# Trial matrix products of 64 rows, in pairs on the two halves of the array, behind the last projection

## The chip, the cores and the metric

The kernel runs on one core of one Trainium2 chip. That core has a matrix engine (PE, an array of 128 rows by 128 columns, which loads a 128-column weight tile and then streams up to 512 columns of a second operand past it), a vector engine (DVE), a scalar engine (ACT), a third elementwise engine (POOL), and a queue that issues most of the transfers (SP). Products are summed in PSUM, which has 8 banks of 128 partitions by 512 float32.

The metric is the time of one execution on the device in microseconds. Two executions of the kernel before took 689.73 and 689.46 us, a median of 689.6 us. The profile shown below belongs to the second of them.

## The reference

The result is the sum of the input, an attention branch and a gated feed-forward branch, both fed from the same layer norm. There are 2048 tokens of width 448, 16 heads of 28, four segments of 512 tokens, and a hidden width of 1792.

```
xn = layernorm(x)
# branch A: softmax attention inside each of 4 segments, plus a recurrent memory over the segments
q, k, v = xn @ wq, xn @ wk, xn @ wv                  # 16 heads of 28
for s in range(4):
    p = softmax(q_s @ k_s.T * scale + mask)          # mask falls on keys behind the query
    o_s = g * (phi(q_s) @ M) / (phi(q_s) @ z + 1e-6) + (1 - g) * (p @ v_s)
    M, z = M + phi(k_s).T @ v_s, z + sum(phi(k_s))
A = o @ wo
# branch B
B = (sigmoid(xn @ w_gate) * (xn @ w_up)) @ w_down
return x + A + B
```

## The kernel before

Every dense product is made to float32 accuracy from operands split in two: a high part rounded to the type `float32r`, and a low part with the rest. A product is then summed from terms high x high, high x low and low x high. The contraction of 448 is cut into three chunks of 128 and one of 64; of the last one the transposed activations hold the high part on partitions 0 to 63 and, beside it, on partitions 64 to 127, the same chunk's low part. With that packing one dense product takes the 11 terms of the table `TERMS`: nine for the three whole chunks and two for the packed one. Each term is one matrix product over all 128 rows of the array, and the 11 add up in one PSUM bank (`start` on the first, `stop` on the last).

`xs[b]` holds the split and transposed activations of token block b: 128 partitions, 7 slices of 512 columns. There are four such tiles. At the end of the program, `split_tokens` has overwritten them with the attention's output.

The work comes in this order. A front part makes the layer norm, the values (`pv`, line 335), the keys and queries (`pp`, line 355) and the memory. Then the feed-forward branch (`pgu`, line 247; `pd`, line 173) and the attention (scores `st`, line 612; weighted values `pa`, line 687) run interleaved on the matrix engine, in an order that the program writes out by hand for PE and SP (`tc.manual_schedule(engines=MANUAL)`). Last comes `project()`: the output projection `po` (line 771), 16 groups of 11 terms, each of 448 columns. Behind each group DVE adds the bank to the residual `acc` (line 775) and SP stores 128 tokens to the output (line 776). The last instruction of PE in the program is the eleventh term of the sixteenth `po`.

PSUM is shared out by tags: `"p"` and `"gu"` have two banks each, and `bank(name, tag)` hands them out in turn. The projection takes `"p"` and `"gu"` alternately. A bank that is handed out again is waited for until whoever used it last is done. Two kinds of product in the kernel before don't fill the array: `st` has 84 rows, and `pa` has 32 columns; four `pa` products at a time stand beside each other on four column strips of the array, and go to four strips of partitions in one bank. `pa` has plain float32 operands, for which the engine runs each product as two passes. No product of the kernel before has 64 rows.

Of the kernel before, what the change touches and what calls it, by code (L numbers as in the profile page):

```python
# [16 lines left out]
P = 128  # L17
D = 448
# [4 lines left out]
L = 512  # L23
# [38 lines left out]
def kernel(  # L62
# [11 lines left out]
    V, A, G, T = nc.vector, nc.scalar, nc.gpsimd, nc.tensor  # L74
# [6 lines left out]
    xs = [keep.tile([P, 7, L], F32R, name=f"xs{b}") for b in range(NB)]  # L81
# [194 lines left out]
    with tc.tile_pool(name="front", bufs=2) as sb, tc.manual_schedule(engines=FRONT):  # L276
# [227 lines left out]
        for b in range(NB):  # L504
            last = b == NB - 1
# [23 lines left out]
            for k, c in enumerate((3, 4, 5, 6, 0, 1, 2) if last else range(7)):  # L529
# [34 lines left out]
                n = k - 1 if b == 0 else k + 1  # L564
# [135 lines left out]
    def attention():  # L700
        for n in range(2):
            pairs[n].load()
        units[0].load_values()
        yield
        run, behind = {}, []
        for u in range(len(units) + 1):
            for n in range(2):
                run[n] = pairs[2 * u + n].scores() if u < len(units) else iter(())
            for k, which in enumerate(SLOT):
                if u == len(units):  # L710

                    if k > 9:
                        break
                    which = (None,) * 8 + (2, 3)
                    which = which[k]
                if behind:
                    next(behind.pop(0))
                if which is not None and which < 2 and u < len(units):
                    next(run[which])
                    n = 2 * u + which + 2  # L720
                    if which not in SLOT[k + 1:]:
                        behind += [run[which]] * PARTS
                        if n < len(pairs):
                            pairs[n].load()
                        else:
                            load_sums(n - len(pairs))
                if which == 2 and u > 0:
                    fin = units[u - 1].finish()
                    next(fin)
                    if u < len(units):  # L730
                        units[u].load_values()
                if which == 3 and u > 0:
                    next(fin)
                yield
# [14 lines left out]
    def project():  # L749

        def split_tokens(b, t):
            o3 = sums[b][:, :, t * P:(t + 1) * P]
            A.activation(xs[b][:, 0:4, t * P:(t + 1) * P], o3, AF.Copy)
            transpose_low(o3, xs[b], t)

        def out_weights(w):
            at = 2 * D * (w // 4) + D * (w % 2)
            return wo[w % 4 // 2][:, at:at + D]

        yield  # L760
        for n in range(NB * NT + 2):
            if n < NB * NT:
                b, t = divmod(n, NT)
                split_tokens(b, t)
                if t == NT - 1 and b + 2 < NB:
                    load_sums(b + 2)
            if n >= 2:
                b, t = divmod(n - 2, NT)
                po = bank("po", ("p", "gu")[n % 2])
                for m, (a, w) in enumerate(TERMS):  # L770
                    T.matmul(po[:, :D], xs[b][:, a, t * P:(t + 1) * P], out_weights(w),  # L771
                             start=m == 0, stop=m == len(TERMS) - 1)
                    if m in (3, 7):
                        yield
                V.tensor_add(acc[b][:, t, :], po[:, :D], acc[b][:, t, :])
                nc.sync.dma_start(out[b * L + t * P:b * L + (t + 1) * P, :], acc[b][:, t, :])
                yield
                if rest:
                    yield from rest.pop(0)

    N_OUT = 1 + NB * NT * 3 + 12
    steps = attention()
    n_att = len(units) * len(SLOT) + 10
    done = 0
    with tc.manual_schedule(engines=MANUAL):
        next(steps)
        k = sum(FILLS) + 6
        for part in (ffn, project()):
            for _ in part:
                want = min(round(n_att * (k - LEAD) / (N_FFN + N_OUT - LEAD - TAIL)), n_att)  # L790
                k += 1
                while done < want:
                    next(steps)
                    done += 1


def _rows(w):
# [36 lines left out]
```

## Time and profile before

| | |
|---|---|
| time of the profiled execution | 689.46 us |
| span from its first to its last instruction | 687.7 us |
| so outside the span | 1.8 us |
| PE busy | 681.7 us, 99% of the span, 3594 matrix products |
| DVE, ACT, POOL busy | 567.4, 342.6, 151.3 us |
| granted clock of PE | 0.999 of full speed |

Of the matrix engine the profile has two rows per product: PE is the streaming, PEld is the load of its weight tile, which goes on beside the product before. A record of PE is longer than the place it takes in the row of products: products are pipelined, so their records overlap, and what one costs is the distance between starts of neighbours. Names in a row read out<-in; `128*128 128x512` means 128 rows by 128 columns of the array and 512 columns streamed. The lines that carry the argument stand with it below.

### The profile page before, as it was taken

The numbers are of one execution on the slowest core, as the hardware profiler recorded it, in microseconds if no ns is written. First come the engines' busy times: TensorE is split into PE (matmuls) and PEld (weight loads), VectorE is DVE, ScalarE is ACT, GpSimd is POOL, SyncE is SP. The second block draws the span as 40 slices with busy tenths as digits, with TensorE's granted clock in tenths as the row PEclk, the third lists the DMA queues.
The fourth block names the chain that finished last, engine by engine and source line by source line (L and its number), as shares of the span: only waits on it lengthen the run. The fifth ranks groups of instructions, "written<-read, shape, count | busy, mean of one in ns | idle before, by whom it ended". The sixth has DMA issues, their size and how long they took to land.

```text
span 687.7 us, 10438 instructions
## 1 busy us (share of the span) xinstructions
PE 681.7 (99%) x3594; PEld 566.6 (82%) x3594; DVE 567.4 (83%) x994; ACT 342.6 (50%) x563; POOL 151.3 (22%) x349
## 2 busy tenths in 40 slices
PE   8999999999999999999999999999999999999997
PEld 7898888778878787787878878787787878878897
DVE  6765795767788988998898989989898899889863
ACT  4837555343554555543655446454653565446320
POOL 3500020101223222232332222322322322222000
PEclk9999999999999999999999999999999999999999
DMA  7446556696233323243223252314333332423342
GB/s 267 181 150 238 198 214 242 249 330 174 71 94 92 80 86 86 56 128 112 56 64 107 57 141 56 109 47 116 82 94 77 96 71 64 95 79 95 95 153 106
DMA packets 45796, 84.37 MB, mean 123 GB/s; under 512 B 6320, under 2 KB 20400, under 8 KB 45232
## 3 DMA queue, kind: packets, MB, share of 16 engines
q1 hardware_dynamic: 42736, 76.37, 35.8%
q0 software_dynamic: 3008, 7.34, 4.9%
q8 instruction: 28, 0.46, 0.3%
q14 instruction: 24, 0.20, 0.1%
HBM read 51.05 MB, written 32.64 MB: 122 GB/s over the span
## 4 chain that ended last, share of the span: by engine, by line
PE 70%; DVE 14%; issue 9%; POOL 4%; DMA 1%; ACT 1%; SPq 0%; POOLq 0%; ACTq 0%
PE pgu L247 26%; PE pd L173 13%; PE pp L355 10%; PE po L771 5%; PE pv L335 5%; PE st L612 3%; PE pa L687 3%; DVE mx L629 3%; DVE w L666 2%; POOL w L627 2%; DVE acc L174 2%; PE pmm L383 2%; PE n L401 2%; DVE hh L259 1%; DVE mx L633 1%
## 5 line engine op out<-in xcount | busy, mean ns | idle before, releaser
L247 PE MATMUL pgu<-xs,wgu 128*128 128x512 f32 x1232 | 304.1, 394 | 0.0
L247 PEld LDWEIGHTS pgu<-xs,wgu 128*128 128x128 f32 x1232 | 228.2, 188 | 47.4 <-issue 2.2
L173 PE MATMUL pd<-wdn,hh 128*128 128x448 f32 x672 | 156.0, 367 | 0.0
L627 POOL TENSOR_SCALAR_AFFINE_SELECT w<-w 128x256 f32<-128x256 f32 (+1 forms) x160 | 81.2, 509 | 236.4 <-ACT w L616 183.6
L173 PEld LDWEIGHTS pd<-wdn,hh 128*128 128x128 f32 x672 | 122.5, 188 | 12.3 <-issue 0.6
L667 ACT ACTIVATE w<-w 128x1024 f32<-128x1024 f32 (+1 forms) x96 | 87.3, 915 | 65.0 <-DVE w L666 64.2
L666 DVE TENSOR_TENSOR w<-w,mb 128x1024 f32<-128x1024 f32 (+1 forms) x96 | 98.9, 1045 | 0.1
L616 ACT ACTIVATE w<-st 128x512 f32<-128x512 f32 x128 | 74.9, 590 | 45.3 <-PE st L612 44.9
L629 DVE TRANSPOSE_TENSOR_REDUCE mx<-w 128x32 f32<-128x1024 f32 x64 | 79.0, 1235 | 17.0 <-POOL w L627 17.0
L355 PE MATMUL pp<-xs,wqk 128*128 128x512 f32 x308 | 77.7, 401 | 0.0
L174 DVE TENSOR_TENSOR acc<-pd,acc 128x448 f32<-128x448 f32 x112 | 67.1, 599 | 1.2 <-PE pd L173 1.1
L355 PEld LDWEIGHTS pp<-xs,wqk 128*128 128x128 f32 x308 | 56.8, 188 | 13.4 <-issue 2.4
L258 ACT ACTIVATE hh<-sg 128x512 fp32r<-128x512 f32 x56 | 35.2, 628 | 56.4 <-DVE sg L256 49.3
L612 PE MATMUL st<-qk 84*128 84x128 f32 (+3 forms) x256 | 61.9, 312 | 0.0
L255 ACT ACTIVATE sg<-pgu 128x512 f32<-128x512 f32 x56 | 33.2, 594 | 49.4 <-PE pgu L247 49.2
L612 PEld LDWEIGHTS st<-qk 84*128 84x128 f32 x256 | 47.6, 189 | 6.9 <-ACT w L616 0.3
L656 DVE STREAM_TRANSPOSE mb<-top 128x1024 f32<-128x1024 f32 x32 | 39.8, 1242 | 10.5 <-POOL top L653 10.1
L362 DVE TENSOR_TENSOR qk<-pp,qk 128x512 fp32r<-128x512 f32 x28 | 19.3, 688 | 29.8 <-ACT e L360 23.7
L259 DVE SCALAR_TENSOR_TENSOR hh<-sg,hh 128x512 fp32r<-128x512 f32 x56 | 38.7, 691 | 2.6 <-ACT hh L258 2.4
L335 PE MATMUL pv<-wv,xs 128*128 128x448 f32 x176 | 39.6, 376 | 0.4 <-DVE xs L102 0.3
L687 PE MATMUL pa<-w,vv 128*32 128x128 f32 (+3 forms) x512 | 39.7, 436 | 0.2
L256 DVE SCALAR_TENSOR_TENSOR sg<-sg,pgu 128x512 f32<-128x512 f32 x56 | 37.3, 665 | 1.8 <-PE pgu L247 1.6
(100 smaller groups left out, 640.6 us busy)
## 6 DMA issues: line engine op xcount, KB each, us to landing
qk<-qd SPq DMA_DIRECT2D x192, 112.0 KB
qd<-qk SPq DMA_DIRECT2D x28, 512.0 KB
raw<-in_w_ffn SPq DMA_DIRECT2D x14, 512.0 KB
vd<-vst SPq DMA_DIRECT2D x4, 1024.0 KB
vv<-vd SPq DMA_DIRECT2D x16, 256.0 KB
od<-w POOLq DMA_DIRECT2D x16, 256.0 KB, 3.8
sums<-od SPq DMA_DIRECT2D x32, 128.0 KB
out<-acc SPq DMA_DIRECT2D x16, 224.0 KB
```

The costliest lines, as they stand in the source:

```text
L173: T.matmul(pd[:, :D], l, r, start=n == 0, stop=n == len(mms) - 1)
L174: V.tensor_add(acc[b][:, t, :], pd[:, :D], acc[b][:, t, :])
L247: T.matmul(dst, wgu[f][:, w, side * P:(side + 1) * P], xs[b][:, a, :], start=n == 0, stop=n == len(TERMS) - 1)
L335: T.matmul(pv[:, :D], xs[b][:, a, t * P:(t + 1) * P], wv[w], start=n == 0, stop=n == len(TERMS) - 1)
L355: T.matmul(pp, wqk[c][:, w, :], xs[b][:, a, :], start=n == 0, stop=n == len(TERMS) - 1)
L612: T.matmul(st[:, at:at + L - kb * P], self.qk[:KS, 1, h, kb * P:(kb + 1) * P], self.qk[:KS, 0, h, kb * P:], start=True, stop=True)
L616: A.activation(w, st, AF.Copy)
L627: G.affine_select(d, d, pattern=pattern, base=0, channel_multiplier=-1, compare_op=ALU.is_ge, fill=MASK)
L629: V.tensor_reduce(mx[:, 16 * (n - 1):16 * (n + 1)], w3[:, n // 2, :2 * L].rearrange("p (b n) -> p b n", n=32), axis=mybir.AxisListType.X, ...
L666: V.tensor_sub(w, w, m)
L667: A.activation(w, w, AF.Exp, scale=SCALE)
L687: T.matmul(pa[32 * j:32 * j + 32, kb * P:], self.vv[:, kb, 32 * j:32 * j + 32], self.pairs[j // 2].block(j % 2, kb), start=kb == 0, stop=k ...
```

## The change

A function `trials()` is added and called once, behind the loops that issue everything else. It issues matrix products on PE and nothing on any other engine. Their weights are slices of `xs[1]`, their streamed operand slices of `xs[0]`, and their results stay in PSUM: nothing reads them, and the output is computed as before.

There are 17 blocks. Nine of them (`ta`, `tc`, `te`, `tg`, `ti`, `tk`, `tm`, `to`, `tq`) are made by `plain`: four products over all 128 rows, into one bank. The eight between them are made by `halves`: pairs of products of 64 rows, one of each pair on rows 0 to 63 and one on rows 64 to 127, each half with a bank of its own. The blocks of halves differ in how many pairs they have, in the width (512 or 448 columns), in the offset of the streamed slices (0, 16 or 32 columns), in whether the lower or the upper half comes first (`swap`), and in whether they use one pair of banks or two in turn.

```
+    def trials():
+        f0, f1 = (xs[b].rearrange("p c n -> p (c n)") for b in range(2))
...
+        def col(cols, k, off=0):
+            at = off + k % (6 if cols == L else 7) * cols
+            return f0[:, at:at + cols]
+
+        def wt(k):
+            return f1[:, k % 27 * P:k % 27 * P + P]
+
+        def plain(name, tag, reps, cols=L):
+            o = bank(name, tag)[:, :cols]
+            for n in range(reps):
+                T.matmul(o, wt(n), col(cols, n), start=n == 0, stop=n == reps - 1)
+
+        def halves(name, plan, cols=L, off=0, swap=False):
+            tags = ("gu", "p", "gu", "p") if len(plan) > 1 else ("gu", "p")
+            outs = [bank(name, t)[:, :cols] for t in tags]
+            reps, last, k = {}, {}, 0
+            for n, a, b in plan:
+                for o in (a, b):
+                    reps[o] = reps.get(o, 0) + n
+            seen = dict.fromkeys(reps, 0)
+            for n, a, b in plan:
+                begun = dict(last)
+                for m in range(n):
+                    for h in ((1, 0) if swap else (0, 1)):
+                        o = (a, b)[h]
+                        r = slice(64 * h, 64 * h + 64)
+                        i = T.matmul(outs[o], wt(2 * k + h)[r], col(cols, k, off)[r],
+                                     start=seen[o] == 0, stop=seen[o] == reps[o] - 1).ins
+                        if m == 0 and o in begun:
+                            tc.add_manual_dep(i, begun[o].name, sync, reason="half")
+                        seen[o] += 1
+                        last[o] = i
+                    k += 1
+
+        whole = ((11, 0, 1), (11, 2, 3))
+        plain("ta", "p", 4)
+        halves("tb", ((16, 0, 1),))
+        plain("tc", "p", 4)
+        halves("td", whole)
+        plain("te", "p", 4)
+        halves("tf", whole, swap=True)
+        plain("tg", "p", 4)
+        halves("th", ((16, 0, 1),), L, 16)
+        plain("ti", "p", 4)
+        halves("tj", ((16, 0, 1),), L, 32)
+        plain("tk", "p", 4, D)
+        halves("tl", ((14, 0, 1),), D, 0)
+        plain("tm", "p", 4, D)
+        halves("tn", ((14, 0, 1),), D, 16)
+        plain("to", "p", 4, D)
+        halves("tp", ((4, 0, 1),))
+        plain("tq", "gu", 4)
...
+        trials()
```

The order of the other engines stays what it was. On PE, all new rows stand between the last projection and the end of the program. The first of them (`x32` counts products, so 16 pairs):

```order
 L771 MATMUL po<-wo,xs_67 128x448 x44
 L771 MATMUL po<-wo,xs_68 128x448 x44
-L830 UNCONDITIONAL_BRANCH
+L797 MATMUL ta<-xs_65,xs_66 128x512 x4
+L813 MATMUL tb<-xs_65,xs_66 128x512 x32
+L797 MATMUL tc<-xs_65,xs_66 128x512 x4
+L813 MATMUL td<-xs_65,xs_66 128x512 x44
+L797 MATMUL te<-xs_65,xs_66 128x512 x4
+L813 MATMUL tf<-xs_65,xs_66 128x512 x44
+L797 MATMUL tg<-xs_65,xs_66 128x512 x4
```

Nothing in front of `ta` has moved; the program's end on PE now stands behind 284 more products (36 plain ones, 248 of halves).

Inside a block of halves, PE's row in the changed kernel alternates between the two banks of a pair. This is the place in `td` where the second pair of banks takes over (the numbers at the names are those of the banks' tiles: 7092 and 7094 belong to rows 0 to 63, 7093 and 7095 to rows 64 to 127; a wait named PE is one for a product that this engine itself issued earlier):

```order
L813 MATMUL td_7092<-xs0_65,xs1_66 128x512
L813 MATMUL td_7093<-xs0_65,xs1_66 128x512
L813 MATMUL td_7094<-xs0_65,xs1_66 128x512
L813 MATMUL td_7095<-xs0_65,xs1_66 128x512 [waits PE_49]
L813 MATMUL td_7094<-xs0_65,xs1_66 128x512
L813 MATMUL td_7095<-xs0_65,xs1_66 128x512
```

The bank of 7095 was last written by `tc`, 22 products earlier. There are 17 such waits in the new rows, each for a bank whose last product lies at least four products back.

More of the change, by code (lines that the diff above doesn't have):

```diff
@@ L779, in project @@
                     yield from rest.pop(0)
+    def trials():
+        f0, f1 = (xs[b].rearrange("p c n -> p (c n)") for b in range(2))
+        sync = mybir.DependencyInfo(mybir.DependencyClass.Sync, mybir.DependencyReason.DATA)
+        def col(cols, k, off=0):
[46 more added lines that the diff above has]
+        plain("tq", "gu", 4)
     N_OUT = 1 + NB * NT * 3 + 12
```

## The prediction

> **What bounds the kernel now.** I read the page first, then the chain of work that ended last near its end, then single rows of the timeline. The page's line of busy times and its line of the granted clock:
>
> ```profile
> PE 681.7 (99%) x3594; PEld 566.6 (82%) x3594; DVE 567.4 (83%) x994; ACT 342.6 (50%) x563; POOL 151.3 (22%) x349
> PEclk9999999999999999999999999999999999999999
> ```
>
> PE is busy almost throughout and its clock is granted in full from end to end. What the change appends comes at the end, so that is the place to read. The chain of work that ended last, from 640 us to the end (start, length, engine, line, count):
>
> ```profile
> 641.46 1.21 PE pd L173 x6
> 642.66 2.29 PE pa L687 x32
> 644.96 2.41 PE po L771 x11
> ...
> 651.96 2.20 PE po L771 x11
> 654.16 1.20 PE pd L173 x6
> ...
> 662.16 22.01 PE po L771 x110
> 684.17 0.02 issue
> 684.20 0.62 DVE acc L775
> ```
>
> The chain at the end is PE alone: product behind product, without a wait. 110 products of 448 columns take 22.01 us, 0.200 us each. PE sets the end until 684.17. Whatever is appended to PE's row starts there and moves the end, except for what lies beside the tail that follows anyway. That tail:
>
> ```profile
> 683.80 0.36 PE L771 MATMUL po<-wo,xs 128*128 128x448 f32 x1
> 684.20 0.62 DVE L775 TENSOR_TENSOR acc<-po,acc 128x448 f32<-128x448 f32 x1 [1.57 <-PE po L771]
> ...
> 684.85 0.33 SPq L776 DMA_DIRECT2D out<-acc  x1
> ...
> SPq L830 <- DMA out<-acc: 1.2, 1, 1.2
> ...
> L830 SPq DRAIN  x3: 7/7/7, 686.9 to 687.2; - x3
> ...
> L830 PEldq DRAIN  x2: 13/1900/3788, 680.4 to 687.3; - x2
> L830 DVEq DRAIN  x2: 19/342/664, 684.2 to 687.3; - x2
> ```
>
> The last product starts at 683.80. Then come the add, the issue of the store, 1.2 us of waiting for it to land, and the closing, whose first drain on SP is at 686.9 and which PE and DVE take part in (their second drains stand at 687.3); the span ends at 687.7.
>
> **What a product costs.** A stretch of the timeline in the middle of the program, and a longer run of full products from the chain:
>
> ```profile
> 265.29 0.40 PE L612 MATMUL st<-qk 84*128 84x512 f32 x1
> 265.53 2.67 PE L247 MATMUL pgu<-xs,wgu 128*128 128x512 f32 x11
> 268.03 0.40 PE L612 MATMUL st<-qk 84*128 84x384 f32 x2
> ...
> 19.99 7.51 PE pp L355 x33
> ```
>
> Full products of 512 columns: 7.51/33 = 0.228 us each, and from 265.53 to 268.03 it is 2.50/11 = 0.227. The `st` row is the nearest one to a product with fewer rows: 84 rows, 512 columns, and the next product starts 0.24 us later. So leaving rows out makes a single product no cheaper. A half product of 64 rows alone is to be priced at a full place; only a second one beside it can save anything.
>
> **Do two stand beside each other?** No row of before has 64 rows. The nearest rows are those of `pa`, four column strips side by side:
>
> ```profile
> 318.13 0.56 PE L173 MATMUL pd<-wdn,hh 128*128 128x448 f32 x2
> 318.62 0.64 PE L687 MATMUL pa<-w,vv 128*32 128x512 f32 x4
> ...
> 318.62 0.16 PEld L687 LDWEIGHTS pa<-w,vv 128*32 128x32 f32 x8 [0.30 <-issue]
> ...
> L687 PE MATMUL pa<-w,vv x32: 272/432/617, 318.6 to 320.7; 128*32 128x512 f32 x8, 128*32 128x384 f32 x8, 128*32 128x256 f32 x8, 128*32 128x128 f32 x8
> ```
>
> Four products whose records are 0.617 us long at most lie within 0.64 us: they start almost together. The 32 passes stream 8 x (512 + 384 + 256 + 128) = 10,240 columns; in turn, at 0.228 us per 512, that would be 4.6 us, and the chain has 2.29 for all of them. So products on different strips of the array do run at once, and their weight loads too (eight loads in 0.16 us). I carry this over from column strips to row halves. What it doesn't show: the strips of `pa` write to different partitions of one bank, while two row halves write the same 128 partitions, of two banks. That open point is the main rival. Bounds for a pair of 512 columns: 0.228 us when they run together, 0.456 when one follows the other; I take 0.228, since `pa` is the only row with more than one product on the array.
>
> The weight loads bound it from another side:
>
> ```profile
> 304.33 0.19 PEld L612 LDWEIGHTS st<-qk 84*128 84x128 f32 x1
> 304.51 0.19 PEld L173 LDWEIGHTS pd<-wdn,hh 128*128 128x128 f32 x1
> ...
> 304.51 0.30 PEld L173 LDWEIGHTS pd<-wdn,hh 128*128 128x128 f32 x2
> ```
>
> Here a load has only a short product (128 columns) to hide behind. Two loads of 0.19 us fill 0.30, so the second starts 0.11 us after the first: a load blocks the next one for 0.11 us. Two loads per pair, one after the other, are 0.22 us. That is hidden behind 0.228 of a pair of 512, and just not behind 0.200 of a pair of 448. For the latter I take 0.218, between 0.200 (loads at once, as in `pa`) and 0.400 (no pairing).
>
> **Changing between whole and halved array.** `pa` again, by the chain and the rows above. Going in: the second `pd` starts at 318.13 + 0.20 = 318.33, and `pa` 0.29 later instead of 0.20, 0.09 more. Coming back: the 11 products behind `pa` take 2.41 us where 11 usually take 2.20, 0.21 more. Together 0.30 us for a round trip; bounds nothing (if row halves switch for free) and twice as much, 0.60. I take 0.30. Eight round trips make 2.4 us. [...]
>
> **The 17 waits of PE for itself.** Before has them too: the order lists one at the `pd` that the chain shows at 654.16, and its six products take 1.20 us like the others. So they are costed at nothing, covered by the four or more products in between (0.9 us); if that cover failed, each could cost the rest of a record, 0.36 - 0.20 = 0.16 us, 2.7 us in all. Nothing else is queued behind these waits, as nothing follows the trials but the program's end, and no other engine reads them.
>
> **The sum,** against the profiled execution (span 687.7, time 689.46, which is 0.1 under the median of 689.6):
> - plain: 24 of 512 by 0.228 = 5.47 us, 12 of 448 by 0.200 = 2.40;
> - pairs: 96 of 512 by 0.228 = 21.89, 28 of 448 by 0.218 = 6.10;
> - eight round trips: 2.4. Together 38.3 us.
>
> The first trial product can start at 683.80 + 0.20 = 684.0 (its bank was added up one group earlier), the last place ends at 722.3. The add, the store and its landing (684.20 to 686.9) now lie beside it and are free; a result that was the end becomes cover worth 2.9 us. Behind the last product come the rest of its record, 0.17 us (a `pgu` record is 394 ns on the page, its place 228), and the closing, from SP's wait just ahead of 686.9 to 687.7, 0.9 us. The closing can't be earlier: the program's end is a meeting of all engines. New span 722.3 + 0.2 + 0.9 = 723.4, 35.7 us more; time 689.46 + 35.7 = 725.2 us, 5.2% over before. The groups on the page for these two numbers:
>
> ```profile
> L247 PE MATMUL pgu<-xs,wgu 128*128 128x512 f32 x1232 | 304.1, 394 | 0.0
> ```
>
> **Rivals.**
> 1. *The halves run one after the other.* If two products can't write the same partitions of two banks at once, each half takes a full place: 192 by 0.228 + 56 by 0.200 = 55.0 us in place of 28.0, 27 us more: 752 us. For it: no row shows two products writing the same partitions, and `st` shows that few rows alone save nothing. Against it: `pa`. Something between (a shared path that slows pairs by a third, say) gives 732 to 748.
> 2. *The load can't hide behind its own half.* If the weights of a half can only be loaded once that half's product is through, each of the 124 pairs shows one load of 0.11 us: 13.6 us more, 739 us. For it: that a halved array keeps a second set of weights per half is shown by no row with 64 rows. Against it: in `pa` the loads of the second passes lie inside those 0.16 us, while the first passes still run. [...]
> 3. *Not slower: products that nobody reads are not carried out.* The place is the end of PE's row. The 2.9 us of cover and the 2% of the measurement (13.8 us) together hide 16.7 us of PE's row, some 73 places of 0.228 in place of the 160 that I count; under that the kernel is not slower. With none carried out the time is 689.5. Against it: all 284 stand in the built program's order, 36 plain ones alone take 7.9 us, and nothing in the profile of before shows PE leaving out a product that stands in its row.
>
> **How the numbers follow.** Two percent, 13.8 us, is about what a measurement of this kernel can tell from no change. Forecast (pairs run together): 0.76, from 721 (switching free, 448 at 0.200, closing a little shorter) to 731 (switching at 0.60, waits at 2.7). Halves in turn, 752: 0.12. Loads in the open, 739: 0.06. Something between, 732 to 748: 0.05. Not slower: 0.01. The time named is that of the likeliest, 725.2. A range from 721 to 740 holds the forecast, the loads in the open and part of what lies between, some 0.84. All cases but the third rival are over 2% slower; that leaves 0.985 for slower, 0.01 for no difference, 0.005 for faster.
>
> **What would show it.** In the profile of the changed kernel: (a) the two products of a pair start within some hundredths of a microsecond, and pairs follow each other every 0.23 us; starts of halves 0.228 apart each would be the first rival, pairs every 0.34 the second. (b) Pairs of 448 every 0.22 rather than 0.20. (c) The first plain product behind a block of halves 0.2 us late, eight times. (d) `ta` starts at 684.0, and DVE's last add and the last store lie beside `ta` and `tb`; the span ends about 1.1 us after PE's last product. (e) Up to 684 nothing has moved, and the clock stays granted in full. The prediction is wrong if blocks of halves differ clearly from each other by offset, order or banks: I forecast the same place for all of them at equal width, as nothing in the trace of before sets them apart.

## The result, and the profile after

The changed kernel takes 725.67 us (725.57 to 725.77, two runs) against 689.6 before: 1.0525 times as long, 95% interval 1.0503 to 1.0546. The forecast was 725.2 us, so the direction, the size and the mechanism came out. Some of its terms did not, and they cancelled in part; the sections below take them apart.

The page's line of busy times, and the line of the core's span and granted clock:

```profile
PE 720.7 (100%) x3878; PEld 595.4 (82%) x3878; DVE 567.7 (78%) x994; ACT 342.5 (47%) x563; POOL 151.4 (21%) x349
core 0: 724.1 us, clock 1.000
```

PE is busy 39.0 us longer than before (681.7) and has 284 products more; the span is 36.4 us longer (724.1 against 687.7). DVE's, ACT's and POOL's busy times are what they were. The chain of work that ended last, from the end of the projection on (start, length, engine, tile, line, count; `tb` counts 31, as one of its 32 half products does not stand on the chain):

```profile
684.22 0.93 PE ta L797 x4
685.15 3.85 PE tb L813 x31
689.00 1.13 PE tc L797 x4
690.13 5.21 PE td L813 x44
...
702.84 3.87 PE th L813 x32
706.71 1.12 PE ti L797 x4
707.83 3.92 PE tj L813 x32
...
712.76 3.08 PE tl L813 x28
...
716.85 3.01 PE tn L813 x28
...
722.00 1.12 PE tq L797 x4
```

The chain is nothing but the trial blocks. `td` has 44 half products in 5.21 us, 0.237 us a pair with what its beginning costs. So the two halves run at once. The timeline of PE shows the same at a block's edges:

```profile
684.05 1.09 PE L797 MATMUL ta<-xs,xs 128*128 128x512 f32 x4
685.08 3.92 PE L813 MATMUL tb<-xs,xs 64*128 64x512 f32 x32
688.93 1.20 PE L797 MATMUL tc<-xs,xs 128*128 128x512 f32 x4
690.06 0.50 PE L813 MATMUL td<-xs,xs 64*128 64x512 f32 x2
```

`ta` starts at 684.05, so up to there nothing has moved. The last row is the first pair of `td`, cut off by the window: two records of up to 497 ns each within 0.50 us. DVE's last add and the last store lie beside `ta` and `tb`:

```profile
684.25 0.62 DVE L775 TENSOR_TENSOR acc<-po,acc 128x448 f32<-128x448 f32 x1 [1.58 <-PE po L771]
...
684.91 0.33 SPq L776 DMA_DIRECT2D out<-acc  x1
...
L890 SPq DRAIN  x3: 7/7/7, 723.3 to 723.6; - x3
```

The closing on SP now waits for PE: its drains stand at 723.3 and later, in place of 686.9.

### The profile page after: what moved, and what is told of

Read it like the earlier page. It is cut to its first block, busy times and chain, and to the rows that moved or that the text cites. A ratio compares the mean times of both kernels' runs of the same rounds, so it can differ in the third digit from the quotient of the medians.

```text
span 724.1 us, 11007 instructions
## 1 busy us (share of the span) xinstructions
PE 720.7 (100%) x3878; PEld 595.4 (82%) x3878; DVE 567.7 (78%) x994; ACT 342.5 (47%) x563; POOL 151.4 (21%) x349
## 4 chain that ended last, share of the span: by engine, by line
PE 72%; DVE 13%; issue 8%; POOL 4%; DMA 1%; ACT 1%; SPq 0%; POOLq 0%; ACTq 0%
PE pgu L247 25%; PE pd L173 12%; PE pp L355 10%; PE po L771 5%; PE pv L335 4%; PE st L612 3%; PE pa L687 3%; DVE mx L629 3%; DVE w L666 2%; POOL w L627 2%; DVE acc L174 1%; PE pmm L383 1%; PE n L401 1%; DVE hh L259 1%; DVE mx L633 1%
```

## The experiments

All kernels leave the work up to the last projection as it is and differ in the trial blocks alone. Those with an interval were timed beside the kernel before on the same chip, where its median was 689.5 us (on each of the two chips that were used). The two kernels with blocks of their own, on the changes and on the offsets, were executed once each and are read by their traces alone.

**Is it the pair that saves, and what does a half alone cost?**

```
# one half: the banks, and the loop over the halves
-                for o in (a, b):
+                for o in (a,):
...
-                    for h in ((1, 0) if swap else (0, 1)):
+                    for h in (0,):
```

> Leaves out the upper product of every pair: 124 half products on rows 0 to 63 remain, everything else as in the changed kernel. Theory (the two halves of a pair run at once and share one place): nothing is saved, 725.7 us within 1 us. Rival (halves take turns, or share something): 124 products fewer save up to 27 us, 699 us; if pairs are slowed by a third through sharing, some 717.

Measured: 725.73 us (725.61 to 726.22), 1.0527 times before (1.0511 to 1.0543). Without 124 of the products the time is the same. The chain has the same lengths with half the count:

```profile
685.20 3.85 PE tb L813 x16
...
712.78 3.08 PE tl L813 x14
```

So the second half of a pair costs nothing, within the spread of some tenths of a microsecond, and a half alone costs a full place. Halves in turn, and sharing that slows a pair, are out.

```
# same half: where a product's operands start
-                        r = slice(64 * h, 64 * h + 64)
+                        r = slice(0, 64)
```

> Puts both products of a pair on rows 0 to 63, each still with its own bank. Theory (a half takes a full place, only a product on the other half goes beside it, and a load hides behind a running product of its own half): 96 places of 0.228 and 28 of 0.203 more, 27.6 us: 753 us. If a load can't hide behind its own half, each of the 248 products shows 0.11 us besides: 780 us. If it is the two banks and not the two halves that let products run at once: 725.7.

Measured: 753.22 us (753.20 to 753.36), 1.0925 times before (1.0907 to 1.0943): 27.5 us over the changed kernel, as expected. The chain:

```profile
685.14 7.48 PE tb L813 x32
...
693.75 10.20 PE td L813 x44
```

`td` takes 10.20 us where it took 5.21, although each pair still has its two banks. It is the two halves of the array that let two products run at once. 10.20/44 is 0.232 us per product, with the block's beginning: there is no room for a load of 0.11 us between products on the same 64 rows. The load (a record of 0.184 us in `tb`) hides behind a running product of its own half, which the second rival denied. With that load in the open at each of the 248 products it would have been 780 us by the expectation above, and it is 753.22.

**What do the changes of the array cost?**

```
# whole array: one product over all rows per pair, in the first bank
-                for o in (a, b):
+                for o in (a,):
...
-                    for h in ((1, 0) if swap else (0, 1)):
+                    for h in (0,):
...
-                        r = slice(64 * h, 64 * h + 64)
+                        r = slice(0, P)
```

> Replaces each pair by one product over all 128 rows with the same width and offset, in the first of the two banks. Theory (a pair costs what a whole product costs; changing between whole and halved array costs 0.40 us a round trip by the changed kernel's trace): eight round trips fewer, 3.2 us: 722.5 us. Rival (a pair costs more than a whole product, no cost of changing): the same 725.7 would come from 0.026 us per pair; then this kernel also ends near 722.5, but the blocks in its trace would be shorter by 0.026 us per product, not by 0.40 at their ends.

Measured: 722.56 us (722.15 to 722.85), 1.0479 times before (1.0464 to 1.0495): 3.1 us less than the changed kernel. Its chain:

```profile
685.20 3.65 PE tb L813 x16
688.85 0.91 PE tc L797 x4
689.76 4.99 PE td L813 x22
694.75 0.91 PE te L797 x4
```

`td` is 0.22 us shorter than as pairs, `tb` 0.20, though `td` has 22 products and `tb` 16; and the plain `tc` and `te`, which were not touched, are 0.22 us shorter too. The difference sits at the edges and not in the products, 0.20 to 0.22 us at each. Among the blocks of halves `tl` alone differs by more: it is 0.25 us shorter as whole products (2.83 in this chain), and the last experiment comes back to it.

```
# regrouped: the calls of the blocks
-        plain("ta", "p", 4)
-        halves("tb", ((16, 0, 1),))
...
+        plain("ta", "p", 4)
+        plain("tc", "p", 4)
...
+        halves("tb", ((16, 0, 1),))
+        halves("td", whole)
...
```

> Issues the nine plain blocks first and then the eight blocks of halves: one change of the array in place of sixteen. Theory (0.40 us a round trip): 7.5 round trips fewer, 3.0 us: 722.7 us. Rival (pairs cost more, changing costs nothing): 725.7 us, no change.

Measured: 722.67 us (722.48 to 722.73), 1.0481 times before (1.0465 to 1.0496): 3.0 us less with every product in place. That is 0.40 us for each of the 7.5 round trips left out. The chain:

```profile
684.29 0.93 PE ta L797 x4
685.22 0.93 PE tc L797 x4
686.15 0.91 PE te L797 x4
...
692.22 3.88 PE tb L813 x32
696.10 4.99 PE td L813 x44
701.09 4.99 PE tf L813 x44
```

Only `tb`, which comes first, still pays for a change. `td` takes 4.99 us as 22 pairs, exactly what it took as 22 whole products: a pair costs what a whole product costs, 0.227 us. In this kernel `td` also begins with a wait of PE for itself and has such waits in its middle, and so does `tf`; 4.99/22 leaves no room for any of them.

**Of what does a change consist, and do the loads of a pair run at once?** This kernel has other trial blocks: eight times a pair and a whole product in turn, with weights of 128 columns (`whalf`, `wwhole`) and of 96 (`xhalf`, `xwhole`), and then 20 pairs and 20 whole products of 256 columns (`twohalf`, `twowhole`) and of 128 (`onehalf`, `onewhole`).

```
# other blocks; row() makes n pairs, or with whole=True n whole products
...
+        for a, wcols in (("w", P), ("x", 96)):
+            row(a + "start", 8, L, whole=True, wcols=wcols)
+            for n in range(8):
+                row(a + "half", 1, L, wcols=wcols, start=n)
+                row(a + "whole", 1, L, wcols=wcols, start=n, whole=True)
+        for a, cols in (("two", 256), ("one", 128)):
+            row(a + "half", 20, cols)
+            row(a + "whole", 20, cols, whole=True)
```

> Other trial blocks, read in the trace. First, eight times one pair and one whole product in turn, of 512 columns, with 128 columns of weights, and then the same with 96. Theory (a change shows the whole load of 0.11 us and some 0.09 of draining): one turn takes 2 x (0.228 + 0.11 + 0.09) = 0.86 us with 128 columns, 2 x (0.228 + 0.08 + 0.09) = 0.80 with 96. Rival (a fixed price of changing): 0.86 for both. Then 20 pairs and 20 whole products of 256 columns, and the same of 128 columns. If the two loads of a pair run at once: 0.12 us per pair of 256, 0.11 per pair of 128, as for whole products. If they run in turn, as the prediction assumed: 0.22 us for a pair of either width.

Measured in the chain:

```profile
686.86 0.43 PE whalf L828 x2
...
692.48 0.43 PE wwhole L828
...
694.76 0.41 PE xhalf L828 x2
...
700.86 0.41 PE xwhole L828
701.26 2.59 PE twohalf L828 x40
703.85 2.58 PE twowhole L828 x20
706.43 2.38 PE onehalf L828 x40
708.81 2.38 PE onewhole L828 x20
```

Between the first two rows lie 13 pieces, a pair or a whole product each, between the next two 15; each piece has one change. One takes (692.48 - 686.86) / 13 = 0.432 us with 128 columns and (700.86 - 694.76) / 15 = 0.407 with 96; for a turn of two pieces that is 0.86 and 0.81, where the theory had 0.86 and 0.80. Less the place of a product, 0.228, a change costs 0.20 and 0.18 us. 32 columns fewer save 0.025, 0.8 ns a column; if that goes on in a straight line, a whole load of 128 is 0.10 us of the price, and the other 0.10 don't depend on the weights. The fixed price is refuted. The trace of the changed kernel shows the two parts where `td` follows `tc`:

```profile
689.73 0.40 PE L797 MATMUL tc<-xs,xs 128*128 128x512 f32 x1
...
690.06 0.19 PEld L813 LDWEIGHTS td<-xs,xs 64*128 64x128 f32 x2 [0.36 <-issue]
```

The weight loads were idle for 0.36 us: the loads of `td`'s first pair are not brought forward across the change. They begin 0.33 us after the start of the last product of `tc`, 0.10 after its place of 0.228 is over, and together with the record of `td`'s first pair (690.06 as well). So the load lies inside that record, which is 0.50 us long where most of `td` have 0.39. What takes place in the 0.10 ahead of the load, which the expectation calls draining, no run shows.

Pairs and whole products take the same time at either width: 2.59 us and 2.58 for 256 columns (0.12 us each, less the change), 2.38 for 128 (0.11). In turn, the two loads of a pair would have needed 0.22 us each time, 4.4 us for 20 pairs. They run at once; the row of `td` above shows it too, two loads within the 0.19 us of one.

**How much lies beside the tail?** Only the first block is left, with ten products.

```
-        plain("ta", "p", 4)
-        halves("tb", ((16, 0, 1),))
...
+        plain("ta", "p", 10)
```

> Leaves out all trial blocks but the first, which has ten whole products in place of four (2.3 us of PE's row). Theory (up to about 2.6 us of appended products lie beside the last add, the last store and its landing): 689.6 us, no change, span 687.7. Rival (every appended product counts in full): 691.9 us, span 690.0.

Measured: 689.5 us (689.4 to 689.79), 1.000 times before (0.9991 to 1.0009), span 687.9. 2.31 us of PE's row are free, as they lie beside the last add and the last store:

```profile
684.28 2.31 PE ta L797 x10
```

**Why do blocks of equal width differ?** In the changed kernel `tl` and `tn` have 14 pairs of 448 columns each, and `tl` takes 3.08 us, `tn` 3.01; `tb`, `th` and `tj` have 16 pairs of 512, at 3.85, 3.87 and 3.92. They differ in the offset of the streamed slice. Six pairs of offsets (streamed, weights) in columns of four bytes, a to f, 20 products each: pairs of 448 (`ha` to `hf`) and 512 (`ia` to `if`), whole products of 448 (`ja` to `jf`) and 512 (`ka` to `kf`).

```
+        for a, cols in (("h", D), ("i", L)):
+            for b, (off, woff) in zip("abcdef", ((0, 0), (16, 0), (32, 0), (48, 0), (0, 16), (16, 16))):
+                row(a + b, 20, cols, off, woff)
+        for a, cols in (("j", D), ("k", L)):
+            for b, (off, woff) in zip("abcdef", ((0, 0), (16, 0), (32, 0), (48, 0), (0, 16), (16, 16))):
+                row(a + b, 20, cols, off, woff, whole=True)
```

> Other trial blocks, read in the trace: 20 products per block, as pairs and as whole products, of 448 and of 512 columns, each with six pairs of offsets (streamed slice, weights) in columns: (0, 0), (16, 0), (32, 0), (48, 0), (0, 16), (16, 16). If the start of the streamed slice alone sets the place: the last two blocks equal the first two. If the distance between the weights and the streamed slice sets it: (16, 16) equals (0, 0). If it is a matter of halves: pairs differ by offset and whole products don't. From the changed kernel's trace: pairs of 448 take 0.207 at (0, 0) and 0.200 at (16, 0); pairs of 512 0.2275, 0.229 and 0.232 at 0, 16 and 32.

Measured in the chain (`ha` and `ja` also pay for a change of the array, 0.20):

```profile
684.16 4.32 PE ha L828 x40
688.48 4.00 PE hb L828 x40
...
704.64 4.13 PE hf L828 x40
708.77 4.55 PE ia L828 x40
713.33 4.59 PE ib L828 x40
...
727.21 4.67 PE ie L828 x40
731.87 4.55 PE if L828 x40
736.42 4.25 PE ja L828 x20
...
756.85 4.05 PE jf L828 x20
760.90 4.56 PE ka L828 x20
...
779.35 4.67 PE ke L828 x20
784.01 4.55 PE kf L828 x20
```

Shifting both operands by 16 columns (f) gives back the time of no shift (a): 4.55 and 4.55 for pairs of 512, 4.56 and 4.55 for whole products, 4.13 against 4.32 - 0.20 for pairs of 448. Shifting one alone doesn't: 4.59 and 4.67. So it is the distance between the weights and the streamed slice that sets the place, and not where the stream starts, as far as one shift of both shows it; and it is no matter of halves, since whole products of 512 have the same times (`ie` and `ke` 4.67). These times come back some 50 us later in the run, so they are no drift. Only at 448 columns without a shift do pairs stand a little over whole products (`hf` 4.13, `jf` 4.05). The span of the effect is 2.6% at 512 columns (4.55 to 4.67) and about 3% at 448 in pairs (4.00 to 4.13). Why a distance is good or bad stays open.

## Why the prediction was right, and where a term was off

**Where the appended work goes: right.** PE's row sets the end, `ta` starts at 684.05 (forecast 684.0), and what ended the program before is cover. The forecast put the cover at about 2.6 us of appended products (2.9 less the rest of the last record and the wait); ten products of 2.31 us cost nothing. In the changed kernel the chain's last product ends at 723.1, 1.0 us ahead of the span's end; before, 3.5 us lay between (684.17 to 687.7). So about 2.5 us were free there.

**The place of a pair: right.** This was the term that carried most, 21.9 of 38.3 us, and it was carried over from the column strips of `pa`, on an open point: two products writing the same partitions, in two banks. One half alone takes as long as the pair (725.73 against 725.67), two products on one half take double (753.22), and 22 pairs take what 22 whole products take (4.99 us). The forecast's other branches, 752 for halves in turn and 739 for loads in the open, are not merely missed by the total: each has a kernel against it.

The row that this was carried over from says more than the forecast took from it. It set the 2.29 us of `pa` against 4.6 in turn, by 0.228 us per 512 columns. But `pa` has plain float32 operands, and a pass of those takes longer. The kernel before shows it at `n` (112 rows, so it doesn't fill the array either; plain float32, one product at a time in two passes), and at the second passes of `pa` themselves:

```profile
82.31 1.02 PE L401 MATMUL n<-phi,mst 112*128 112x512 f32 x2
...
82.75 0.59 PE L401 MATMUL n<-phi,mst 112*128 112x512 f32 x1
...
319.07 0.61 PE L687 MATMUL pa<-w,vv 128*32 128x512 f32 x4
...
319.50 0.51 PE L687 MATMUL pa<-w,vv 128*32 128x384 f32 x4
```

The two passes of `n` start 0.43 us apart (1.02 - 0.59). By that price the passes of `pa` in turn would take 20 x 0.43 = 8.6 us, and four strips at once 2.15: the measured 2.29 leaves only the changes over. As the forecast read it, four strips gained a factor of two, which would have left room for its "something between"; the row rightly read leaves little. That two halves can write the same partitions, in two banks, no row of before shows; that point was a bet, and the runs bear it out as far as the time goes (22 pairs in 4.99 us).

**The waits of PE for itself: right,** at nothing: with its waits `td` takes 4.99 us in the regrouped kernel, as 22 whole products do.

**Changing the array: mis-sized.** The forecast took 0.30 us a round trip from `pa`, 2.4 in all; it is 0.40, 3.2 in all. Coming back was right (0.21 forecast, 0.20 measured). Going in was not: 0.09 from `pa`, 0.20 here. The step that failed is the reading of that row. It counted how late the first products of `pa` start; but their load lies inside their own records (both start at 318.62), so it shows only behind them. The second passes start 319.07 - 318.62 = 0.45 us after the first, where a pass takes 0.43 (319.50 - 319.07): 0.02 us more. By the 0.8 ns a column a load of 32 columns is 0.026 us, and `pa` loads 32. So the change into `pa` cost 0.11 to 0.12, of which 0.09 lie ahead of the load; with 128 columns the load alone is 0.10. That the price hangs on the columns, and that `pa` has a quarter of them, was not noticed.

**The loads of a pair: wrong.** The forecast had them in turn, 0.22 us, and took 0.218 for a pair of 448. `tl` and `tn` take (3.08 + 3.01 - 0.40) / 28 = 0.203. The row of the spacing between two loads on the same rows of the array was read rightly; that it holds for loads on different halves was assumed, against `pa`, whose eight loads lay within 0.16 us.

**Equal places for all blocks of equal width: wrong,** by up to 2 or 3%, from the distance of the operands. The forecast named this as what would make it wrong. Of the three things it named there, only the offset matters: with one pair of banks (`tb`), with two (`td`) and with the upper half first (`tf`, 5.23 us for 22 pairs) a pair takes 0.228, 0.228 and 0.229 us, with 0.20 a block taken off for the change. At 512 columns it is worth little here, since the best distance is also that of offset 0.

The terms beside each other, from the chain (the blocks' lengths with 0.20 taken off for each change):

| term | forecast, us | measured, us |
|---|---|---|
| plain, 24 of 512 | 5.47 | 5.56 |
| plain, 12 of 448 | 2.40 | 2.42 |
| pairs, 96 of 512 | 21.89 | 22.0 |
| pairs, 28 of 448 | 6.10 | 5.69 |
| eight round trips | 2.4 | 3.2 |
| sum | 38.3 | 38.9 |
| span | 723.4 | 724.1 |

The two mis-sized terms, 0.8 too little and 0.4 too much, leave 0.4; the rest of the 0.7 in the span is three tenths over the other rows and the closing. That they cancel is luck: with the first alone the forecast would have been off by a microsecond, of 36. The lower end of its range is not borne out by its own terms either: 725.2 less 2.4 (switching free) and 0.5 (pairs of 448 at 0.200) is 722.3, and a closing of 1.1 us cannot be a little shorter by another 1.3.

## What to carry to other kernels

What was appended here behind the last instruction of the engine that sets the end cost its own time less what lies beside the tail: about 2.5 us were free, and everything beyond that counted in full (38.9 us of blocks, 36.4 of span). Two products of 64 rows and 512 columns on the two halves of the array, each with its own bank, took the place of one whole product, 0.227 us, but coming and going cost 0.40 us with 128 columns of weights, as much as 1.75 products of 512 columns (0.40/0.228). An estimate from these numbers: if a kernel could save half a place in each of its groups of products by such a pair (0.114 us), it would have to put four groups between two changes before it gains. What no run here shows is a pair that shares one bank, and whether the sums of the pairs are right, as nothing reads them. Where a price is carried over from another operation, check that what it may depend on (here the columns of weights) is the same in both.

## What the runs showed of the hardware that was not expected

- A change between whole and halved array cost 0.20 us each way with 128 columns of weights and 0.18 with 96: the load is not brought forward across it (0.36 us of idle weight loads ahead of `td`), and 0.10 us lie ahead of the load.
- Weight loads for the two halves of the array run at once: two within 0.19 us, where two on the same rows took 0.30.
- The place of a product changed with the distance between its weights and its streamed slice: 4.55 to 4.67 us for 20 places of 512 columns, pairs and whole products within 0.01 us of each other.
- Some blocks of four plain products of 512 columns took a little more than four times 0.227 us. In the regrouped kernel the first two, `ta` and `tc`, take 0.93 us each and the third, `te`, 0.91. In the changed kernel `tc` and `ti` each follow a change and take 1.13 and 1.12; less 0.20 for the change that is 0.92 to 0.93. Why stays open.
